# Down projection as 26 block products of a 2x4x4 scheme, with hand-placed SBUF slots and a term preset in PSUM by ScalarE

## The chip, the cores and the metric

The kernel runs on one core of a Trainium2 chip. The metric is the device time of one execution in microseconds. Before: 1897.8 us, the median of three runs (1897.66 to 1897.85).

## The reference

```python
x: (8, 3008, 256)                       # fp32
X = fft(fft(x, axis=1), axis=2).real     # sequence, then features
h = X.reshape(24064, 256) @ w_in         # (256, 2048)
g = maximum(0.01 * h, h)                 # leaky relu
out = g @ w_out                          # (2048, 256)
```

All arithmetic is fp32. The feature transform is linear and is folded into the input weights, so that the kernel computes a cosine and a sine transform along the sequence, and then two projections.

## The kernel before, in words

**Units and chunks.** A unit is one batch entry and one parity of the output frequency (16 units of 752 or 753 frequencies). Each frequency k gives two output rows, k and its mirror, which are the sum and the difference of a cosine half and a sine half. A unit is cut into chunks of 251 or 250 frequencies, 48 in all. The features d and 256 - d are folded, so the cosine and the sine half have 128 features each, and the feature d = 128 is a term of its own: the row `nb` (spread over all partitions) times a weight column `wn`.

**Up.** A step (chunk j, index f of 8) makes two hidden blocks of 128 features. `raised` (L820) issues four matmuls into two PSUM banks, `cos_ps` and `sin_ps`. `activate` then adds the d = 128 term on VectorE (L829, nb times wn plus cos_ps, to SBUF), makes the sum and the difference with sin_ps (L833, L834: the two mirrored rows of `g`), and applies Lrelu on ScalarE (L835). GpSimd makes four sums of column blocks (L842 to L845, tile `s`).

**Down.** `down` (L893) multiplies by a 2x2x2 scheme with seven products for each f, accumulated over all eight f in four PSUM banks. The weights of the products are blocks of w_out (`wo`) and four differences of them (`wt`, made on GpSimd in L601). When the last f is done, seven additions on VectorE (L917) and a copy on ScalarE (L902) make the output tile `o`, and two transfers store it. The first two chunks are "plain" (`down_plain`, L873: eight products for each f), since w_out is still arriving then.

**Sequence transform.** For the next unit, VectorE folds x (L327 to L343) and its rows (L363 to L410) and TensorE makes two groups of eight small matmuls of 94 to 96 columns (L635, `even_rows`, `odd_rows`); `butterfly` puts the parts together on VectorE into the tiles `mix0` and `mix1`, of which there are two each. `dft_direct` does the same for the second unit from the layout of the first load.

**Order.** TensorE and SyncE (SP) follow the order of the program text everywhere, VectorE too but for steps 16 to 22. `step(at)` issues up of step `at` and down of step `at - 3`; folds and transforms are tied to steps by the tables `folds`, `row_folds` and `transforms`. PSUM is two rings of four banks: `up` (also for transforms) and `sum`. SBUF tiles come out of pools with a number of buffers for each tag: five of `g`, four of `s`, two of `o`, two of `nb`. Loads of x, tables and output stores are all issued on SP.

Of the kernel before, what the change touches and what calls it, by code (L numbers as in the profile page):

```python
# [45 lines left out]
SLOPE = 0.01  # L96
# [148 lines left out]
def chunks():  # L245


    out, at = [], 0
    for b in range(B):
        for c in PARITIES:  # L250
            for j in range(0, UW[c], CW):
                n = min(CW, UW[c] - j)
                out.append((b, c, j, n, at))
                at += 2 * n
    return out, at


def columns():

    at = np.zeros(B * S, np.int64)  # L260
    for b, c, j, n, first in chunks()[0]:
        col = j + np.arange(n)
        half, k = col >= KW[c], k_order(c)
        k = np.concatenate([k, k[k != Q]])[col]
        plus, minus = np.where(half, H + k, k), np.where(half, H - k, (S - k) % S)
        at[b * S + minus] = first + n + np.arange(n)
        at[b * S + plus] = first + np.arange(n)
    return at
# [3 lines left out]
def tile_fnet_leaky_relu(  # L272
# [16 lines left out]
    PS = bass.MemoryType.PSUM  # L289
    const = ctx.enter_context(tc.tile_pool(name="const", bufs=1))  # L290
    xp = ctx.enter_context(tc.tile_pool(name="xp", bufs=1))
    work = ctx.enter_context(tc.tile_pool(name="work", bufs=1))
    dram = ctx.enter_context(tc.tile_pool(name="dram", bufs=1, space=bass.MemoryType.DRAM))
    ps = ctx.enter_context(tc.tile_pool(name="ps", bufs=1, space=PS))

    def up_ps(name="up_ps"):
        return ps.tile([P, 512], F32, tag="up", bufs=4, name=name)

    def dft_ps():
        return up_ps("dft_ps")  # L300

    def x_tile():
        return xp.tile([LOADED, 2, 2, NT, D], F32, tag="x", bufs=1, name="xt")

    def sum_ps():
        return ps.tile([P, 512], F32, tag="sum", bufs=4, name="sum_ps")

    def load_x(b):
        t = x_tile()
        for h in range(2):  # L310
            for odd in range(2):
                load_rows(t, b, h, odd)
        return t

    def load_rows(t, b, h, odd):
        nc.sync.dma_start(t[:, h, :, odd * NI[0] : NI[0] + odd * NI[1]], x[b, h, odd])
# [4 lines left out]

    zs = {}
# [22 lines left out]
    def fold_x(b, at):  # L345

        t, rows = xs[b], slice(0, NT)
        h, i = divmod(at, 2)
        if h < 2 and i == 0:
            add_mirrors(t, h, rows)  # L350
        elif h < 2:
            for part in range(2):
                fold_columns(t, h, part, rows)
        else:
            fold_halves(t, i, 3 - h, rows)
        if at == 7:
            zs[b] = xs.pop(b)

    def turn(x, y, a, part, tmp, to, v):
# [3 lines left out]
        nc.scalar.activation(tmp[0], y, ACT.Copy, scale=sin)  # L363
        nc.scalar.activation(tmp[1], y, ACT.Copy, scale=cos)
        if v is nc.vector:
            v.scalar_tensor_tensor(to[0], in0=x, scalar=cos, in1=tmp[0], op0=ALU.mult, op1=op[part])
            v.scalar_tensor_tensor(to[1], in0=x, scalar=sin, in1=tmp[1], op0=ALU.mult, op1=op[1 - part])
            return
        nc.scalar.activation(to[0], x, ACT.Copy, scale=cos)
        nc.scalar.activation(to[1], x, ACT.Copy, scale=sin)  # L370
# [3 lines left out]
    class Rows:  # L374
# [12 lines left out]
        def fold_even(self, v=nc.vector):  # L387
            x, y, z = self.src[:, 2], self.src[:, 3], self.z
            if self.c == 1:
                turn(x, y, 0, self.part, (z(0), z(1)), (z(6), z(7)), v)  # L390
# [6 lines left out]
        def fold_odd(self, v=nc.vector):  # L397
            x, y, z = self.src[:, 4:6], self.src[:, 6:8], self.z
            if self.c == 1:
                for i in range(2):  # L400
                    turn(x[:, i], y[:, i], 1 + i, self.part, (z(2 + 2 * i), z(3 + 2 * i)), (z(8 + 2 * i), z(9 + 2 * i)), v)
# [3 lines left out]
            else:  # L405
# [5 lines left out]
                turn(z(b), z(b + 1), 0, self.part, (z(8), z(9)), (z(10), z(11)), v)  # L411
                self.odd = z(7 - self.part), z(6 + self.part), z(10), z(11)

    def rows_of_x(b, part, c):

        t = zs[b]
        src = t[:, (c + part) % 2, 0, :, part * P : (part + 1) * P]
        return Rows(src, [t[:, part, 1].rearrange("p c (i d) -> p (c i) d", i=2)], part, c)

    class Direct:  # L420
# [14 lines left out]
        def odd_rows(self, m, lo=0, hi=KW[1]):  # L435

            po, n = dft_ps() if m == P else sum_ps(), KW[1]
# [26 lines left out]
    rows_of = {}  # L464

    def fold_rows(u, part, odd):
        if not odd:
            rows_of[u, part] = rows_of_x(u[0], part, u[1])
            rows_of[u, part].fold_even()
        else:  # L470
            rows_of[u, part].fold_odd()


    feat_sb = const.tile([P, 2, 2 * P], F32, name="feat_sb")
    wf = const.tile([P, 2, F], F32, name="wf")
    wn = const.tile([P, NF], F32, name="wn")
    wo = const.tile([P, 2, NH, D], F32, name="wo")
    wt = const.tile([P, 4, NH, P], F32, name="wt")
    nyx = const.tile([LOADED, 2, 2, NT, B], F32, name="nyx")
    nyz = const.tile([LOADED, 16, B], F32, name="nyz")  # L480
    nyf = const.tile([LOADED, 2, 2, 2 * FI, B], F32, name="nyf")
# [6 lines left out]
    def load_tab(n, c):  # L488
        t = const.tile([LOADED, TW[c][n % 2]], F32, name=f"tab_{n}_{c}")
        nc.sync.dma_start(t, seq_tab[n, c, :, 0 : TW[c][n % 2]])  # L490
        tabs[n, c] = t
# [4 lines left out]
    class Weights:  # L496
# [7 lines left out]
        def __init__(self, src, dst):  # L504
            tag = RAW[len(parts)]
            bufs = 1 if tag == "raw" else 2
            words = src.shape[1] * src.shape[2]
            self.raw = work.tile([P, 2 * WN], F32, tag=tag, bufs=bufs, name="raw")[:, 0:words]
            self.dst, self.n = dst, dst.shape[1]
            self.f64 = src.dtype != F32  # L510
            raw = self.raw if not self.f64 else self.raw.bitcast(src.dtype)
            nc.sync.dma_start(raw.rearrange("p (c n) -> p c n", c=src.shape[1]), src)
            parts.append(self)
# [4 lines left out]
        def begin(self):  # L518
# [3 lines left out]
            self.power = work.tile([P, WN], F32, tag="power", bufs=2, name="power")[:, 0 : self.n]  # L522
# [40 lines left out]
    def load_w_in(f0, n, blocks=(0, 1)):  # L563
        words, made = w_in.shape[1] // F, []
        for a in blocks:
            w = work.tile([P, WN], F32, tag="win", bufs=4, name="win")[:, 0:n]
# [4 lines left out]
    def fold_w_in(f0, n, made, tag="up", pieces=1, queue=nc.sync):  # L571


        for w in (1, 0):
            m = n // (1 if w else pieces)
            for at in range(0, n, m):
                pt = ps.tile([P, 512], F32, tag=tag, bufs=4, name="wf_ps")[:, 0:m]
# [12 lines left out]
    def load_w_out(q):  # L590

        src = w_out[q * WB * P : (q + 1) * WB * P, :].rearrange("(c p) d -> p c d", p=P)
        h, f = divmod(q * WB, NH)
        return Weights(src, wo[:, h, f : f + WB, :].rearrange("p c d -> p (c d)"))

    def combine_w_out(f):

        b = [[wo[:, h, f : f + WB, i * P : (i + 1) * P] for i in range(2)] for h in range(2)]
        t = [wt[:, i, f : f + WB, :] for i in range(4)]
        for to, x, y in ((t[0], b[0][1], b[0][0]), (t[1], b[1][1], t[0]), (t[2], b[1][1], b[0][1]), (t[3], b[1][0], t[1])):  # L600
            nc.gpsimd.tensor_tensor(to, x, y, op=ALU.subtract)  # L601
# [37 lines left out]
    def butterfly(to, m, part, c, v=nc.vector, direct=False):  # L639
# [4 lines left out]
        def tile_of(tag, w, bufs=1):  # L644
            return work.tile([P, w], F32, tag=tag, bufs=bufs, name=tag)

        if not direct or v is not nc.vector:
            od = tile_of("od", 568)
        if v is nc.vector:
            ab, ev = tile_of("ab", KC), tile_of("ev", KC, 2)  # L650
# [14 lines left out]
        def copied(bank, at, w):  # L665

            a = work.tile([P, 384], F32, tag="e0", bufs=2, name="e0")
            if v is nc.vector:
# [28 lines left out]
        def added(po, lo=0, hi=kw):  # L697
            if c == 0:
                for lo, hi in ((0, 189), (189, kw)):
                    at = lo + (lo > 0)  # L700
                    nc.vector.tensor_tensor(to[0:m, lo:hi], ev[0:m, lo:hi], po[0:m, at : at + hi - lo], op=ALU.add)
                return
            nc.vector.tensor_tensor(to[0:m, lo:hi], ev[0:m, lo:hi], po[0:m, 0 : hi - lo], op=ALU.add)

        def subtracted(po, lo=0, hi=kw):
            if c == 0:

                last = 283
                for lo, hi in ((0, 189), (189, last), (last + 1, kw)):
                    at, first = lo + (lo > 0), kw + lo - (lo > last)  # L710
                    nc.vector.tensor_tensor(to[0:m, first : first + hi - lo], ev[0:m, lo:hi], po[0:m, at : at + hi - lo], op=ALU.subtract)
                return
            nc.vector.tensor_tensor(to[0:m, kw + lo : kw + hi], ev[0:m, lo:hi], po[0:m, 0 : hi - lo], op=ALU.subtract)

        def odd(po):
            if c == 1:
# [4 lines left out]
                v.tensor_tensor(to[0:m, 0:kw], ev[0:m, 0:kw], od[0:m, 0:kw], op=ALU.add)  # L721
                v.tensor_tensor(to[0:m, kw : UW[c]], ev[0:m, 0:kw], od[0:m, 0:kw], op=ALU.subtract)
# [8 lines left out]
            v.tensor_tensor(to[0:m, 0:kw], ev[0:m, 0:kw], od[0:m, 0:kw], op=ALU.add)  # L731

            last = 283
            v.tensor_tensor(to[0:m, kw : kw + last], ev[0:m, 0:last], od[0:m, 0:last], op=ALU.subtract)
            v.tensor_tensor(to[0:m, kw + last : UW[c]], ev[0:m, last + 1 : kw], od[0:m, last + 1 : kw], op=ALU.subtract)
# [3 lines left out]
    def mix(u, blk, direct=False):  # L739

        t = work.tile([P, UW[0]], F32, tag=f"mix{blk}", bufs=2, name=f"mix{blk}")
        mixed.setdefault(u, {})[blk] = t
        return butterfly(t, P, blk, u[1], direct=direct)

    def dft(u, blk):
        rows = rows_of.pop((u, blk))
# [420 lines left out]
```

## Time and profile before

| | |
|---|---|
| median of the runs | 1897.8 us |
| span of the profiled execution | 1895.3 us |
| TensorE busy, instructions | 1889.2 us, 9088 |
| plain chunks' up steps end | about 109 us |
| first and last down matmul of the 2x2x2 scheme | 129.7 and 1890.5 us |
| 131 to 1890 us: TensorE, VectorE, ScalarE, GpSimd busy | 1759.0, 1161.4, 446.7, 1032.3 us |

The profiled execution's span lies 2.5 us under the median of the runs. The window from 131 to 1890 us is the steady part; before it, weights are loaded and converted, and the first unit is transformed. A matmul in fp32 appears as two instructions of TensorE. In a group's row the number after the bar is the busy time, then the mean of one instruction in ns, then the idle time of that engine just before these instructions and who ended it. Rows of TensorE have durations with the pipeline's depth in them; a rate is read from the starts.

### The profile page before, as it was taken

How to read it: one execution, taken by the hardware profiler on the slowest of the kernel's cores; microseconds unless marked ns; L12 is line 12 of the kernel's file. 1: busy time of each engine (PE TensorE's matmuls, PEld its weight loads, DVE VectorE, ACT ScalarE, POOL GpSimd, SP SyncE). 2: the span in 40 equal slices, each digit the busy share in tenths (PEclk: the TensorE clock that was granted, in tenths of full speed). 3: DMA queues.
4: the chain of work that ended last, by engine and by line, in shares of the span. 5: the costliest groups of instructions: out<-in, count | busy, mean ns of one | idle time of the engine just before them, and what ended most of it. 6: DMA issues, size and time to landing. Idle time of an engine off the chain costs nothing.

```text
span 1895.3 us, 25288 instructions
## 1 busy us (share of the span) xinstructions
PE 1889.2 (100%) x9088; PEld 1682.3 (89%) x9088; DVE 1266.8 (67%) x2543; ACT 501.0 (26%) x674; POOL 1055.5 (56%) x1510
## 2 busy tenths in 40 slices
PE   9999999999999999999999999999999999999999
PEld 7888888988889888898888988889888898888987
DVE  8857765776656776568756687567865677656554
ACT  3522322223222222222222232222322223222222
POOL 0236555565555655556555565555655556555554
PEclk9999999999999999999999999999999999999999
DMA  7312000110002000020000200003000020000000
GB/s 252 114 58 82 12 20 22 51 69 12 31 11 104 16 22 20 12 108 18 16 20 12 108 23 11 20 12 119 12 12 19 17 114 12 20 11 23 12 12 23
DMA packets 34349, 78.74 MB, mean 42 GB/s; under 512 B 5536, under 2 KB 20000, under 8 KB 34224
## 3 DMA queue, kind: packets, MB, share of 16 engines
q1 hardware_dynamic: 33792, 76.86, 10.9%
q8 instruction: 73, 1.20, 0.3%
q14 instruction: 52, 0.43, 0.1%
q10 hardware_dynamic: 432, 0.26, 0.0%
HBM read 52.40 MB, written 24.71 MB: 41 GB/s over the span
## 4 chain that ended last, share of the span: by engine, by line
PE 99%; DVE 0%; issue 0%; ACT 0%; DVEq 0%; POOL 0%; POOLq 0%
PE sum_ps L893 58%; PE sin_ps L820 17%; PE cos_ps L820 17%; PE sum_ps L873 3%; PE dft_ps L635 3%; PE wf_ps L579 1%; PE sum_ps L956 1%; PE dft_ps L431 0%; PE dft_ps L440 0%; PE sum_ps L440 0%; PE dft_ps L458 0%; PE dft_ps L453 0%; DVE cos L829 0%; PE sum_ps L788 0%; DVE wo L545 0%
## 5 line engine op out<-in xcount | busy, mean ns | idle before, releaser
L835 ACT ACTIVATE g<-g 128x1004 f32<-128x1004 f32 (+1 forms) x384 | 399.3, 1040 | 1134.6 <-DVE g L834 1114.4
L829 DVE SCALAR_TENSOR_TENSOR cos<-nb,wn,cos_ps 128x251 f32<-128x251 f32 (+1 forms) x768 | 330.5, 472 | 534.1 <-PE cos_ps L820 531.1
L842 POOL TENSOR_TENSOR s<-g 128x251 f32<-128x251 f32 (+1 forms) x368 | 280.5, 762 | 711.4 <-ACT g L835 705.5
L893 PE MATMUL sum_ps<-s,wt 128*128 128x251 f32 (+1 forms) x2208 | 527.6, 374 | 0.0
L893 PEld LDWEIGHTS sum_ps<-s,wt 128*128 128x128 f32 x2208 | 415.9, 188 | 52.3
L820 PE MATMUL cos_ps<-mix,wf 128*128 128x251 f32 (+1 forms) x1536 | 387.8, 374 | 0.0
L820 PE MATMUL sin_ps<-mix,wf 128*128 128x251 f32 (+1 forms) x1536 | 387.8, 374 | 0.0
L893 PE MATMUL sum_ps<-g,wo 128*128 128x251 f32 (+1 forms) x1472 | 372.8, 375 | 0.0
L820 PEld LDWEIGHTS cos_ps<-mix,wf 128*128 128x128 f32 x1536 | 291.2, 190 | 34.2 <-issue 0.5
L820 PEld LDWEIGHTS sin_ps<-mix,wf 128*128 128x128 f32 x1536 | 290.4, 189 | 34.7
L893 PEld LDWEIGHTS sum_ps<-g,wo 128*128 128x128 f32 x1472 | 277.4, 190 | 31.6
L833 DVE TENSOR_TENSOR g<-cos,sin_ps 128x502 f32<-128x502 f32 (+1 forms) x384 | 260.4, 678 | 52.0 <-DVE cos L829 6.5
L845 POOL TENSOR_TENSOR s<-g,s 128x251 f32<-128x251 f32 (+1 forms) x368 | 259.3, 705 | 28.8
L843 POOL TENSOR_TENSOR s<-s,g 128x251 f32<-128x251 f32 (+1 forms) x368 | 271.9, 739 | 0.0
L834 DVE TENSOR_TENSOR g<-cos,sin_ps 128x502 f32<-128x502 f32 (+1 forms) x384 | 257.5, 671 | 0.0
L844 POOL TENSOR_TENSOR s<-g 128x251 f32<-128x251 f32 (+1 forms) x368 | 256.2, 696 | 0.0
L893 PE MATMUL sum_ps<-s,wo 128*128 128x251 f32 (+1 forms) x736 | 215.8, 375 | 0.0
L893 PE MATMUL sum_ps<-g,wt 128*128 128x251 f32 (+1 forms) x736 | 215.7, 375 | 0.0
L893 PEld LDWEIGHTS sum_ps<-s,wo 128*128 128x128 f32 x736 | 139.5, 190 | 16.3
L893 PEld LDWEIGHTS sum_ps<-g,wt 128*128 128x128 f32 x736 | 139.8, 190 | 15.8
L917 DVE TENSOR_TENSOR o<-e,sum_ps 128x251 f32<-128x251 f32 (+1 forms) x180 | 66.0, 408 | 0.0
L873 PE MATMUL sum_ps<-g,wo 128*128 128x251 f32 x256 | 57.1, 374 | 0.5 <-DVE wo L545 0.5
(130 smaller groups left out, 802.8 us busy)
## 6 DMA issues: line engine op xcount, KB each, us to landing
xt<-in_x_dram SPq DMA_DIRECT2D x28, 1024.0 KB, 7.6
out_dram<-o SPq DMA_DIRECT2D x78, 251.0 KB, 2.3
raw<-in_w_in_dram SPq DMA_DIRECT2D x8, 512.0 KB, 5.8
raw<-in_w_out_dram SPq DMA_DIRECT2D x8, 512.0 KB, 4.5
out_dram<-o SPq DMA_DIRECT2D x16, 250.0 KB, 2.1
xt<-in_first_x_dram SPq DMA_DIRECT2D x4, 768.0 KB, 8.4
nb<-nyq_dram SPq DMA_DIRECT2D x8, 376.5 KB, 3.4
nb<-nyq_dram SPq DMA_DIRECT2D x7, 376.0 KB, 4.5
```

The source lines that it names most:

```text
L820: nc.tensor.matmul(pt[blk][:, h * n : (h + 1) * n], lhsT=wf[:, blk, fs[h] * P : (fs[h] + 1) * P], rhs=mixed[b, c][blk][:, at : at + n], st ...
L829: nc.vector.scalar_tensor_tensor(cos[:, hs], in0=spreads[b, c][:, at : at + n], scalar=wn[:, fs[h] : fs[h] + 1], in1=pt[0][:, hs], op0=ALU ...
L833: nc.vector.tensor_tensor(g[:, 0], cos[:, 0 : 2 * n], pt[1][:, 0 : 2 * n], op=ALU.add)
L834: nc.vector.tensor_tensor(g[:, 1], cos[:, 0 : 2 * n], pt[1][:, 0 : 2 * n], op=ALU.subtract)
L835: nc.scalar.activation(g, g, ACT.Lrelu)
L842: nc.gpsimd.tensor_tensor(s1, a[1][0], a[1][1], op=ALU.add)
L843: nc.gpsimd.tensor_tensor(s2, s1, a[0][0], op=ALU.subtract)
L844: nc.gpsimd.tensor_tensor(s3, a[0][0], a[1][0], op=ALU.subtract)
L845: nc.gpsimd.tensor_tensor(s4, a[0][1], s2, op=ALU.subtract)
L873: nc.tensor.matmul(sums[j][d][:, r * n : (r + 1) * n], lhsT=wo[:, fs[h] // NH, fs[h] % NH, d * P : (d + 1) * P], rhs=a[r][h], start=(f == ...
L893: nc.tensor.matmul(sums[j][p], lhsT=still[p], rhs=moving[p], start=(f == 0 and i % 2 == 0), stop=(f == NH - 1), skip_group_check=True)
L917: nc.vector.tensor_tensor(to, x, y, op=ALU.add)
```

## The change

- **Down.** A chunk and the next one of equal width are taken together, as a "four": 31 in all, 22 of width 188, eight of 189, one of 125. Their four column blocks (two chunks, two mirrored rows) by four row blocks of the hidden layer by two halves of the output are multiplied with 26 products in place of 32. Each product is four matmuls (g = 0 to 3), and all four stand next to each other in the list. 28 sums of hidden blocks (table `SUMS`) are made on GpSimd, each over all four g at once; 18 sums of weights (`W_SUMS`) once, on GpSimd. Two results of products share a PSUM bank; there are three banks for them. As soon as a bank is complete, `combine` copies some of it on ScalarE and adds the rest on VectorE (34 additions a four), and the eight outputs are stored one by one.
- **Up.** One stage of `Four.up` is one block of 128 hidden features over both chunks of the four (376 or 378 columns): two matmuls. `seed` has ScalarE write nb times wn into the cos bank ahead of the matmul, two stages early; the matmul then adds to it. ScalarE copies the cos bank to SBUF; VectorE makes the sum and the difference with the sin bank (`hidden`), each straight into two slots; ScalarE applies Lrelu, in place.
- **Memory.** `block_sb` has 23 slots of 4 x 189 columns for hidden values and their sums, handed out by a free list in the order of the program; `part_sb` has 22 for outputs. The same memory holds the buffers of the start. x takes three parts of eight rows in place of four, and the tables of the transform are loaded anew for each unit. `mix` and `nb` become rings of three halves.
- **Order.** All five engines follow the order of the program text, from the start to the end. `rest` makes one list of events with due times in "steps" (16 to a four): up at 1.6 + 0.9 f, sums at the times of `SUMS`, products at 17 + m/6.5. VectorE's combinations (`soon`) and folds (`later`) are queued and given out by `spare` in front of and after each up stage, some 0.8 us at a time.
- **Last four.** Every third sum is on VectorE.

```diff
+    def seed(self, f):
+        n = 2 * self.n
+        nc.scalar.activation(cos_ps[f % 2][:, 0:n], columns_of(nb_sb, ...), ACT.Copy, scale=wn[:, f : f + 1])
+    def up(self, f):
+        for i, bank in enumerate((cos, sin)):
+            nc.tensor.matmul(bank[:, 0:n], lhsT=wf[:, i, f * P : (f + 1) * P], rhs=columns_of(mix_sb[i], ...),
+                             start=(i == 1), stop=True, skip_group_check=True)
...
+        nc.scalar.copy(copy, cos[:, 0:n])
+    def hidden(self, k, g, copy, sin):
+        cols = slice(g * n, (g + 1) * n)
+        for r in range(2):
+            a, b = self.at[4 * k + r], self.at[4 * k + 2 + r]
+            step = b - a
+            end = b + (1 if step > 0 else -1)
+            tos.append(block_rows[:, a : (None if end < 0 else end) : step, cols])
...
+        for to, op in zip(tos, (ALU.add, ALU.subtract)):
+            nc.vector.tensor_tensor(to, x, y, op=op)
+    def sum(self, i, engine=None):
+        x, y, sign, _ = SUMS[i]
+        free = [s for s in (self.used(x), self.used(y)) if s is not None]
+        self.at[16 + i] = free.pop(0) if free else block.take()
+        (engine or nc.gpsimd).tensor_tensor(self.value(16 + i), xa, ya, op=ALU.add if sign > 0 else ALU.subtract)
+        for s in free:
+            block.drop(s)
...
+    def product(self, q, g):
+        nc.tensor.matmul(to, lhsT=weight(w)[:, g], rhs=self.value(v)[:, g * n : (g + 1) * n],
+                         start=(first and at == 0), stop=(last and g == 3), skip_group_check=True)
...
+            else:
+                made = four.up(i)
+                seed(16 * t + i + 2)
+                spare(0.8)
+                for to in four.hidden(*made):
+                    nc.scalar.activation(to, to, ACT.Lrelu)
+                spare(0.9)
-        nc.vector.scalar_tensor_tensor(cos[:, hs], in0=spreads[b, c][:, at : at + n], scalar=wn[...], in1=pt[0][:, hs], ...)
-        nc.vector.tensor_tensor(g[:, 0], cos[:, 0 : 2 * n], pt[1][:, 0 : 2 * n], op=ALU.add)
-        nc.vector.tensor_tensor(g[:, 1], cos[:, 0 : 2 * n], pt[1][:, 0 : 2 * n], op=ALU.subtract)
-        nc.gpsimd.tensor_tensor(s1, a[1][0], a[1][1], op=ALU.add)
-        nc.gpsimd.tensor_tensor(s2, s1, a[0][0], op=ALU.subtract)
-        nc.gpsimd.tensor_tensor(s3, a[0][0], a[1][0], op=ALU.subtract)
-        nc.gpsimd.tensor_tensor(s4, a[0][1], s2, op=ALU.subtract)
```

## Prediction

> **What bounds the kernel now.** I read the page's busy times and slices first, then the groups, then the waits, then two stretches of the timeline.
>
> ```profile
> PE 1889.2 (100%) x9088; PEld 1682.3 (89%) x9088; DVE 1266.8 (67%) x2543; ACT 501.0 (26%) x674; POOL 1055.5 (56%) x1510
> ...
> PEclk9999999999999999999999999999999999999999
> ```
>
> TensorE never rests and has its full clock. A matmul in fp32 stands as two instructions ("passes"); the end of the chain, 54 passes of 251 columns in 11.47 us, gives 0.212 us a pass. The prices of other widths come from three rows of the TensorE timeline, by their starts:
>
> ```profile
> 114.83 0.80 PE L453 MATMUL dft_ps<-direct,xt 128*128 128x380 f32 x2
> 115.47 0.81 PE L458 MATMUL dft_ps<-direct,xt 126*128 126x188 f32 x4
> 116.12 1.01 PE L820 MATMUL cos_ps<-mix,wf 128*128 128x250 f32 x4
> ```
>
> Two passes of 380 take 0.64, so 0.32 each; four of 188 to 192 take 0.65, so 0.16 each. Narrow passes aren't held up by their weight loads.
>
> ```profile
> L835 ACT ACTIVATE g<-g 128x1004 f32<-128x1004 f32 (+1 forms) x384 | 399.3, 1040 | 1134.6 <-DVE g L834 1114.4
> L829 DVE SCALAR_TENSOR_TENSOR cos<-nb,wn,cos_ps 128x251 f32<-128x251 f32 (+1 forms) x768 | 330.5, 472 | 534.1 <-PE cos_ps L820 531.1
> L842 POOL TENSOR_TENSOR s<-g 128x251 f32<-128x251 f32 (+1 forms) x368 | 280.5, 762 | 711.4 <-ACT g L835 705.5
> ...
> L834 DVE TENSOR_TENSOR g<-cos,sin_ps 128x502 f32<-128x502 f32 (+1 forms) x384 | 257.5, 671 | 0.0
> ```
>
> The other engines wait for each other in a ring, and it costs nothing: GpSimd waits 706 us for Lrelu, ScalarE 1114 us for VectorE, VectorE 531 us for TensorE. One turn of it:
>
> ```profile
> 608.92 0.67 DVE L834 TENSOR_TENSOR g<-cos,sin_ps 128x500 f32<-128x500 f32 x1
> 609.70 1.04 ACT L835 ACTIVATE g<-g 128x1000 f32<-128x1000 f32 x1 [4.88 <-DVE g L834]
> ...
> 610.82 0.63 POOL L842 TENSOR_TENSOR s<-g 128x250 f32<-128x250 f32 x1 [2.79 <-ACT g L835]
> ```
>
> A hand-over costs about 0.1 us (609.59 to 609.70, 610.74 to 610.82). The changed kernel depends on how dear GpSimd is:
>
> ```profile
> L842 POOL TENSOR_TENSOR s<-g 128x251 f32<-128x251 f32 x304 | 240.3, 791 | 560.5 <-ACT g L835 560.5
> ...
> L601 POOL TENSOR_TENSOR wt<-wo 128x256 f32<-128x256 f32 x8 | 5.8, 728 | 34.9 <-DVE wo L545 34.9
> ...
> L406 POOL TENSOR_TENSOR nyz<-nyx 95x16 f32<-95x16 f32 x1 | 0.2, 217 | 0.0
> ```
>
> From 16 to 256 elements it rises by 511 ns: 2.13 ns an element over 0.18 us.
>
> [...] of one L842 shape the median is 711 ns and the mean 791; over all 1472 sums the excess is 53 us for 143 us of overlap with such instructions, 0.37 us for each. [...]
>
> **The change on TensorE.** After the two plain chunks, before has 46 chunks of 88 matmuls: 1716 us (8096 passes by 0.212). After has 31 "fours". Down: 2288 matmuls of 188 columns, 832 of 189, 104 of 125; two passes each, at 0.160 (0.112 for 125): 1021 us. Up: 704 of 376, 256 of 378, 32 of 250: 621 us with 0.317 and 0.212. Sum 1642, so TensorE loses 74 us. The sequence transform is unchanged. A four of 188 costs 208 x 0.160 + 64 x 0.317 = 53.5, with its share of the transform (16 passes at 0.111) 55.3 us.
>
> **VectorE and ScalarE.** VectorE loses the wn products (L829) and gets per four 32 TENSOR_TENSOR of 376 from PSUM at 0.54 (between 0.409 for 251 in L917 and 0.675 for 502), 34 combinations at 0.345, and its old folds: about 37 of 55 us. ScalarE gets 16 seeds (about 0.6), 16 copies (0.47, as L789), 32 Lrelus at 0.52 (L835's 1.04 less 628 x 0.82 ns, the slope of its copies), 8 copies: about 39 of 55. Both lie beside TensorE if each is in time. Output goes out as 8 transfers a four in place of 4 in two chunks, on SP, behind table loads; SP is nearly idle and I cost that at nothing (up to 20 us if loads of x land late).
>
> **GpSimd.** It makes 28 sums per four: 607 of 752 elements at 1.785 us, 224 of 756 at 1.79, 28 of 500 at 1.25; together 1520 us. That is 50 of the 55.3 us of a four, so any wait beyond 5 us a four sets the end.
>
> **The waits that the change adds.** I read them from the changed kernel's instruction order. `hidden` writes two slots of one large block with one strided access. Only 80 of the 992 such writes have neighbouring slots; in the others up to 20 slots lie between. The order shows that such a write waits for sums that wrote a slot in between, and such a sum for the Lrelu of slots around it: the stretch counts, not the two slots. So the ring of before comes back between fours that share no data. At 202 of the 859 sums GpSimd's next sum waits for a Lrelu whose TENSOR_TENSOR pair waited for the sum just before; nothing else stands between the two in GpSimd's order. The price of one: 0.54 + 0.54 + 0.52 and four hand-overs (0.35) = 1.95 us where it waits for the first Lrelu (71 places), 2.5 for the second (131). In 10 of them a whole further up stage lies between (copy 0.47, two TENSOR_TENSOR, two Lrelu, hand-overs: 2.95). Sum 138 + 328 + 30 = 496 us. At 60 more places one sum can run meanwhile: about 35 us. Behind GpSimd wait the products, then the PSUM banks; behind VectorE's waiting write stand combinations and folds (1.2 us an up stage), which fit beside the sums that run then.
>
> **Start, contention, end.** The plain steps end at 109 us (L820). Their two last downs take 7; then 15 ups of the first four, with nothing to overlap, go at 0.37 + 2 x 0.41 + 2 x 0.42 + 0.35 = 2.4 us each, and dft_direct and the Nyquist rows stand between: first sum at about 155. VectorE's two-SBUF work is about 300 us; with 80% of it over sums, at 0.37: 85-90. Fours in which TensorE is the longer: 20. Last products, combinations, store: 6.
>
> Sum: 155 + 1520 + 496 + 35 + 87 + 20 + 6 = 2319 us of span. The profiled execution before has a span of 1895.3 against a median of 1897.8; with that 2.5, 2320.
>
> **Bounds.** Sums: among the 251s some operand offsets give 630 ns, others 718. At the fast rate a 752 costs 1.52, in all 230 us less. I take the slow one[...]. Contention: 40 to 170. Start: 145 to 170. A hand-over of 0.05 or 0.15: 40 us either way. Side work on VectorE that isn't covered: 0 to 240.
>
> **Rivals.**
> - *TensorE still sets the end* (faster). One mechanism: the waits are in time, because GpSimd runs ahead. It decides if they cost under 5.3 us a four. For it: a product stands about 1.5 ups after its sum. Against it: 496 us over 30 fours is 16.5. It gives 1897.8 - 74, plus 12 for the start that overlaps nothing and 5 at the end (sums are late when no ups are left): 1841.
> - *Fast sums*: 2320 - 230 = 2090. For it: 432 of the 1472 present sums run at that rate (L844 of the 251s, two lines of the 250s). Against it: L601's 728.
> - *The ring catches side work too*: VectorE's 1.2 us per up stage comes in the way at each of the 202 places: 2320 + 242 = 2560. Against it: only some 80 of 480 stages hold more than the sums beside them cover.
> - *The change doesn't do what it says*: the order shows 26 x 4 products a four, so no.
>
> **Numbers.** Forecast 0.69; fast sums 0.10; more of the ring 0.13; TensorE-bound 0.06; something near the old time 0.02. The range, 2080 to 2500, takes in the fast sums and leaves out the TensorE-bound case and half of the worst one. Slower by over 0.2% (what a measurement can tell from none) 0.93, faster 0.05, same 0.02.
>
> **What would show it.** TensorE busy at about 75%, its idle time ended by GpSimd's sums; GpSimd as the longest engine at 1.6 ms or more, waiting some 500 us for Lrelu; Lrelu waiting for the TENSOR_TENSOR pair and this for sums; a sum of 752 at 1.8 us; passes of 188 at 0.16. The forecast is wrong if TensorE is again at 99%, or if GpSimd's idle time is under 150 us.

## The result and the profile after

| | |
|---|---|
| median of the runs, before and after | 1897.8 and 2449.0 us |
| ratio after/before, 95% interval | 1.290 [1.288, 1.292] |
| span of the profiled execution after (its own time 2446.3) | 2444.6 us |
| forecast, range | 2320, 2080 to 2500 us |

The change makes the kernel 29% slower. The page of the changed kernel first; its rows answer to the busy times and slices shown of before.

```profile
PE 2025.6 (83%) x9424; PEld 1659.9 (68%) x9424; DVE 1573.0 (64%) x2820; ACT 1130.4 (46%) x2490; POOL 1606.7 (66%) x900
...
PEclk9998999989999898988998989999998988899999
```

TensorE is no longer full (83% against 100%), and its clock, at nine tenths or more in every slice before, now falls in many slices (mean 0.925). No engine is full: something makes them take turns. The groups of the changed kernel say who waits (busy time and mean ns of one, then the idle time ahead and who ended it):

```profile
L1038 POOL TENSOR_TENSOR block<-block 128x752 f32<-128x752 f32 (+2 forms) x859 | 1576.0, 1853 | 741.7 <-ACT block L1208 535.1 <-PE sum_psc L1053 76.6 <-PE cos_psb L999 42.2
L1208 ACT ACTIVATE block<-block 128x376 f32<-128x376 f32 (+2 forms) x992 | 495.9, 514 | 837.4 <-DVE block L1021 824.5 <-ACT block L1208 0.4
L921 DVE TENSOR_TENSOR part<-part 128x188 f32<-128x188 f32 (+2 forms) x403 | 381.2, 970 | 4.3
...
L1021 DVE TENSOR_TENSOR block<-cos,sin_psb 128x376 f32<-128x376 f32 (+2 forms) x496 | 258.2, 539 | 313.2 <-POOL block L1038 230.2 <-PE sin_psb L999 39.8 <-ACT cos L1006 38.2
```

GpSimd's sums wait 535 us for Lrelu, Lrelu 825 us for VectorE's pair of writes, the pair for sums: the ring that was harmless before is closed, and this time with TensorE outside it. From the waits of the changed kernel (us in total, times, longest):

```profile
ACT block L1208 <- DVE block L1021: 824.5, 466, 7.9
POOL block L1038 <- ACT block L1208: 535.1, 224, 8.3
DVE block L1021 <- POOL block L1038: 377.0, 186, 4.9
...
PE sum_psc L1053 <- POOL block L1038: 200.3, 76, 7.5
```

TensorE's products wait at the end of it. One turn of the ring in the timeline of the changed kernel, GpSimd, then VectorE, then ScalarE (start, duration):

```profile
1284.90 3.50 POOL L1038 TENSOR_TENSOR block<-block 128x752 f32<-128x752 f32 x2 [2.40 <-ACT block L1208]
1290.86 10.69 POOL L1038 TENSOR_TENSOR block<-block 128x752 f32<-128x752 f32 x6 [2.46 <-ACT block L1208]
```

```profile
1288.44 1.12 DVE L1021 TENSOR_TENSOR block<-cos,sin_psb 128x376 f32<-128x376 f32 x2 [3.98 <-POOL block L1038]
```

```profile
1289.66 1.06 ACT L1208 ACTIVATE block<-block 128x376 f32<-128x376 f32 x2 [3.86 <-DVE block L1021]
```

The sums end at 1288.40; the pair of additions takes 1288.44 to 1289.56, the pair of Lrelus 1289.66 to 1290.72, and the next sum starts at 1290.86, after 2.46 us in which GpSimd does nothing. The forecast had 2.5 for this place. Where a sum waits for the first Lrelu alone, the gap is 1.85 us (at 1325.93 and 1338.70 in the same stretch); the forecast had 1.95.

The sums' records add up to the span: the first starts at 150.0 us, all 859 on GpSimd take 1592 us, the gaps between them, less 16 us of overlap, 697 us, and 6.5 us follow the last one: 2445.

### The profile page after: what moved, and what is told of

It reads as the page before. It is cut to its first block, busy times and chain, and to the rows that moved or that the text cites. A ratio compares the mean times of both kernels' runs of the same rounds, so it can differ in the third digit from the quotient of the medians.

```text
span 2444.6 us, 27317 instructions
## 1 busy us (share of the span) xinstructions
PE 2025.6 (83%) x9424; PEld 1659.9 (68%) x9424; DVE 1573.0 (64%) x2820; ACT 1130.4 (46%) x2490; POOL 1606.7 (66%) x900
## 5 line engine op out<-in xcount | busy, mean ns | idle before, releaser
L1038 POOL TENSOR_TENSOR block<-block 128x752 f32<-128x752 f32 (+2 forms) x859 | 1576.0, 1853 | 741.7 <-ACT block L1208 535.1
L1208 ACT ACTIVATE block<-block 128x376 f32<-128x376 f32 (+2 forms) x992 | 495.9, 514 | 837.4 <-DVE block L1021 824.5
L1021 DVE TENSOR_TENSOR block<-cos,sin_psb 128x376 f32<-128x376 f32 (+2 forms) x496 | 258.2, 539 | 313.2 <-POOL block L1038 230.2
L1021 DVE TENSOR_TENSOR block<-cos,sin_psa 128x376 f32<-128x376 f32 (+2 forms) x496 | 257.4, 537 | 260.9 <-POOL block L1038 146.8
L1053 PE MATMUL sum_psa<-block,wt 128*128 128x188 f32 (+2 forms) x1736 | 342.0, 334 | 54.3 <-POOL block L1038 53.9
L921 DVE TENSOR_TENSOR part<-part 128x188 f32<-128x188 f32 (+2 forms) x403 | 381.2, 970 | 4.3
L1053 PEld LDWEIGHTS sum_psa<-block,wt 128*128 128x128 f32 x1736 | 296.8, 196 | 117.1 <-POOL block L1038 71.5
L1053 PE MATMUL sum_psc<-block,wt 128*128 128x188 f32 (+2 forms) x1736 | 324.1, 329 | 48.7 <-POOL block L1038 48.5
L1053 PEld LDWEIGHTS sum_psc<-block,wt 128*128 128x128 f32 x1736 | 290.2, 195 | 82.6 <-POOL block L1038 57.7
L999 PE MATMUL cos_psa<-mixc,wf 128*128 128x376 f32 (+2 forms) x496 | 209.1, 505 | 2.1 <-ACT cos_psa L993 2.1
```

Source lines behind the costliest of these rows:

```text
L921: self.push(n / 960 + 0.15, lambda: nc.vector.tensor_tensor(to, x, y, op=op), tag)
L999: nc.tensor.matmul(bank[:, 0:n], lhsT=wf[:, i, f * P : (f + 1) * P], rhs=columns_of(mix_sb[i], self.u, self.j, n), start=(i == 1), stop=Tr ...
L1021: nc.vector.tensor_tensor(to, x, y, op=op)
L1038: (engine or nc.gpsimd).tensor_tensor(self.value(16 + i), xa, ya, op=ALU.add if sign > 0 else ALU.subtract)
L1053: nc.tensor.matmul(to, lhsT=weight(w)[:, g], rhs=self.value(v)[:, g * n : (g + 1) * n], start=(first and at == 0), stop=(last and g == 3), ...
L1208: nc.scalar.activation(to, to, ACT.Lrelu)
```

## The experiments

**Theory.** The ring through falsely shared stretches of the block memory sets the time: a strided access over two slots is ordered against everything between the slots, so sums, pair writes and Lrelus of unrelated data wait in turn. **Rivals**: the waits are those of real data (a sum needs its Lrelu) and stay when the stretches are gone; or the sums themselves, with what they do to VectorE, set the time.

The first four kernels change the stretches; the two cuts also make more and shorter instructions of the same work. The cut of the Lrelu (A) and the cut of the pair write (B):

```diff
 A           for to in four.hidden(*made):
-                nc.scalar.activation(to, to, ACT.Lrelu)
+                for i in range(2):
+                    nc.scalar.activation(to[:, i], to[:, i], ACT.Lrelu)
 B           for to, op in zip(tos, (ALU.add, ALU.subtract)):
-                nc.vector.tensor_tensor(to, x, y, op=op)
+                for i in range(2):
+                    nc.vector.tensor_tensor(to[:, i], x[:, i], y[:, i], op=op)
```

**Cut A alone: Lrelu slot by slot.**

> The Lrelu over a pair of slots is cut into two, one slot each (1984 in place of 992; the same work otherwise). In the instruction order 92 in place of 320 sums then wait for a Lrelu, and none of the 202 places is left where a sum waits for a Lrelu whose TENSOR_TENSOR pair waited for the sum just before. My theory (the ring of waits over stretches between slots): GpSimd's 535 us of waiting for Lrelu go, its waits for TensorE stay at most as they are (139 us), TensorE's clock returns: 1850 to 1930 us, although ScalarE has some 190 us more to do. Rival, GpSimd's 28 sums a four are too many in themselves: its 1592 us stay and other waits take the place, 2300 us or more. Rival, ScalarE's queue (seed, copy, Lrelu) is what is late: slower than 2449 us, since it gets more instructions.

Measured: 2289.1 us, ratio 1.206 [1.204, 1.208]. The theory's number was missed by over 350 us. The waits of this kernel say why:

```profile
ACT block L1209 <- DVE block L1021: 653.3, 451, 8.9
POOL block L1038 <- DVE block L1021: 400.4, 238, 6.0
```

Sums no longer wait for Lrelu, but they wait for VectorE's pair of additions, whose output has the very same stretch. One cut shortens each turn by the Lrelu (400.4 / 238 = 1.68 us in place of 535.1 / 224 = 2.39), and the ring stays closed.

**Cut B alone: pair write slot by slot.**

> Only VectorE's sum and difference are cut into one slot each; the Lrelu keeps the pair. The order still has 195 of the 202 places, since the Lrelu of the pair waits for the sum. My theory: the ring stands, no gain, 2430 to 2520 us (VectorE has 0.15 us more at 32 places a four, in the ring). Rival, it is VectorE's wait for GpSimd (377 us) that costs: 2100 us or less.

Measured: 2282.6 us, 1.204 [1.201, 1.206]; faster than the theory's range by some 150 us, and far from the rival's. Now the Lrelu pair alone keeps the ring, also with shorter turns (1.74 us on the mean, without the 30.1 us ahead of the very first sum):

```profile
POOL block L1039 <- ACT block L1209: 418.7, 224, 30.1
...
ACT block L1209 <- POOL block L1039: 168.7, 137, 3.7
```

**Both cuts.**

> Both cut. None of the 202 places is left; VectorE and ScalarE both have more instructions. My theory: as with the Lrelu alone within 2%, 1850 to 1940 us. Rival, VectorE's own waits for stretches matter beside the ring: clearly faster than with the Lrelu alone.

Measured: 2105.7 us, 1.110 [1.108, 1.111]. Of all that the change loses (551 us), 343 go with the two cuts; either alone takes some 160. The instruction order of this kernel has none of the 202 places left, and the trace agrees; its waits:

```profile
ACT block L1210 <- DVE block L1022: 528.6, 224, 14.0
POOL block L1039 <- PE sum_psc L1054: 300.9, 68, 8.6
PEld sin_psa L999 <- DVE block L1022: 147.3, 48, 4.7
...
POOL block L1039 <- ACT block L1210: 34.6, 2, 29.5
```

GpSimd waits for Lrelu twice, one of them the first sum of all. So the ring of false waits is real, and cutting it gains 343 us. But the theory's time for this kernel (up to 1940) was missed, and it is clearly faster than with the Lrelu cut alone, as the rival had it: 535 us of waits gone should have given more. Another wait has come in: sums wait for TensorE, whose products have yet to read the slot that the sum goes into; TensorE waits for VectorE's additions to empty its banks. VectorE is 84% busy here, and one group of it has become dear:

```profile
PE 1902.2 (90%) x9424; PEld 1583.7 (75%) x9424; DVE 1774.8 (84%) x3812; ACT 1194.9 (57%) x3482; POOL 1639.9 (78%) x900
```

```profile
L921 DVE TENSOR_TENSOR part<-part 128x188 f32<-128x188 f32 (+2 forms) x403 | 486.2, 1231 | 4.3
```

1231 ns for an addition of 188 columns, where the same with one operand in PSUM takes about 345. That is the second theory: **VectorE's instructions with two SBUF operands are held while GpSimd works**, called the lock theory below (the lock is a name for this holding, no more).

**Near slots: the two slots of a pair taken as close as the free list allows** (82 of the 202 places left).

```diff
-                for j in range(4):
-                    self.at[4 * k + j] = block.take()
+                for r in range(2):
+                    x, y = min(((x, y) for x in block.free for y in block.free if x < y), key=lambda p: p[1] - p[0])
+                    ...
+                    self.at[4 * k + r], self.at[4 * k + 2 + r] = x, y
```

> The four slots of a group are picked from the free ones as two pairs with the fewest slots between; instructions as in the changed kernel. The order has 82 of the 202 places left. My theory: the waits for Lrelu shrink in proportion, by 535 x 120/202 = 318 us, so 2130 us, 2050 to 2200. Rival (the number of instructions on VectorE and ScalarE, or GpSimd's rate, sets the time): 2400 us or more, since neither changes.

Measured: 2259.9 us, 1.191 [1.189, 1.193]; missed by 60 us over the range.

```profile
POOL block L1041 <- ACT block L1211: 367.5, 121, 13.1
```

The waits fall from 224 to 121, but each is longer (3.04 us in place of 2.39). A count of places by one price is not enough once the stages between them shift.

**Near slots, and only the pairs that are not neighbours cut** (508 of 992), to see if the additional instructions of the two cuts cost anything.

> Slots picked as near pairs, and only those pairs cut that aren't neighbours (508 of 992): no false wait is left, with 484 fewer instructions on VectorE and on ScalarE than with all cut. Theory (VectorE sets the end now): its 0.15 us for each of 484 are saved nearly in full, 2020 to 2090 us. Rival, GpSimd or ScalarE sets it: within 1% of 2106.

Measured: 2123.3 us, 1.119 [1.117, 1.121]: within 1% of both cuts, as the rival said. So 484 fewer instructions each on VectorE and ScalarE gain nothing here; the slots differ too, so what the number alone is worth was not measured.

**Both cuts, and sums of 64 columns.** The sum's line becomes `m = 4 * self.n if self.u < 2 else 64` and `tensor_tensor(to[:, 0:m], xa[:, 0:m], ya[:, 0:m])`, so that most columns of the sums are left out.

> Both pairs cut, as in the third experiment, and from the third unit on (28 of 31 fours) GpSimd's sums cover 64 of 752 columns: most of the block sums are left out. Theory now: with the ring gone (2106 us), VectorE is held up, since an instruction of VectorE with two SBUF inputs waits while a sum of GpSimd runs; a part<-part addition of 188 columns took 1572 ns over a sum and 348 ns beside none. Then these fall under 500 ns in the mean, TensorE sets the pace at 55 to 57 us a four, and the time is 1890 to 1960 us. Rival, VectorE's work as such (84% busy, many instructions) holds TensorE up: 2050 us or more.

Measured: 1862.6 us, 0.982 [0.980, 0.983]. The short additions and the full TensorE are as the theory has it; the time lies 28 us under its range. Page and VectorE group of this kernel:

```profile
PE 1826.0 (98%) x9424; PEld 1545.9 (83%) x9424; DVE 1253.6 (67%) x3812; ACT 1226.1 (66%) x3482; POOL 434.7 (23%) x900
```

```profile
L921 DVE TENSOR_TENSOR part<-part 128x188 f32<-128x188 f32 x286 | 97.1, 365 | 3.0
```

With the same order and the same instructions TensorE is full again, and the part additions are back from 1218 ns (188 columns, both cuts) to 365. The waits are not quite the same: a sum of 64 columns touches only the front of its slots, so that in the instruction order 306 of the 859 sums wait for an earlier product or Lrelu than with both cuts. With that reservation, what is left after the two cuts, 243 us, hangs on the sums' length. It doesn't say whether through GpSimd's own time or through what it does to VectorE.

**Both cuts, and each sum in two halves** (`for cols in (slice(0, 2 * self.n), slice(2 * self.n, 4 * self.n))`): the same work on GpSimd, with twice the chances for VectorE to come in between.

> Both pairs cut, and each sum of GpSimd made in two instructions of half the columns (0.18 us more each, 5 us a four on GpSimd). If VectorE waits for the end of the GpSimd instruction that runs, the wait halves with it: a part<-part addition of 188 over a sum falls from 1572 ns to 800 to 1000, and the time to 1930 to 2060 us. Rival, the two engines share the bandwidth and the length of an instruction doesn't matter: 1572 ns stays, and the time is 2106 us or more, up to 2250.

Measured: 2147.3 us, 1.133 [1.130, 1.135]; worse than with whole sums, and in the rival's range. But the rival's 1572 ns did not stay: the usual held addition of 188 columns got shorter (those over 0.4 us have a median of 1.65 us with whole sums and 1.04 here), and 15 of the 403 wait far longer, 205 us of the 502 that all of them take. VectorE and then GpSimd in the timeline of this kernel:

```profile
1081.16 13.69 DVE L921 TENSOR_TENSOR part<-part 128x188 f32<-128x188 f32 x1
1094.77 1.12 DVE L1022 TENSOR_TENSOR block<-cos,sin_psb 128x188 f32<-128x188 f32 x4
```

```profile
1075.79 18.84 POOL L1041 TENSOR_TENSOR block<-block 128x376 f32<-128x376 f32 x20
```

One addition of 188 columns takes 13.69 us: it stands through a run of twenty half sums that follow each other without a gap, and ends with the run (1094.6 and 1094.8). This is not the rule: 284 other part additions that met a half sum ended some 0.21 us after it, with the next half sum following just as closely. What tells the 15 from the 284 stays open. All two-SBUF work of VectorE together takes as long as with whole sums (1017 and 1005 us).

**The changed kernel, ring and all, with VectorE's two-SBUF instructions cut to 8 columns** from the ninth four on (`to, x, y = (a[..., 0:8] for a in (to, x, y))` for parts and x); the other columns of these combinations and folds are left out.

> The changed kernel with its ring (all 202 places), but from the ninth four on VectorE's additions with two SBUF inputs on the output parts and on x cover 8 columns of each row: most of the combination and folding is left out, the number of instructions stays. If VectorE waits for the end of a running sum whatever its own length, these still take over 1 us in the mean over a sum, and the time falls little: 2380 to 2450 us. Rival, the excess over my forecast is the columns that VectorE moves at a shared rate: 2300 to 2350 us, near the sum of the ring.

Measured: 2344.1 us, 1.235 [1.233, 1.237]; the time is the rival's. But the instructions behave as the lock theory has it:

```profile
L925 DVE TENSOR_TENSOR part<-part 128x8 f32<-128x8 f32 x316 | 184.0, 607 | 3.4
```

In their records an 8-column addition takes about 1.0 us on the mean where it lies wholly over sums, and 160 ns beside none, so that 8 columns in place of 188 shorten it by a third only (from 1.45 us). The order of waits on the four computing engines is that of the changed kernel. Against it the sums are 50 us shorter and the gaps 58 us: the columns of VectorE's side work are worth about 105 us in the changed kernel, half of it as longer sums, half as longer waits. The short instructions still wait, and the first eight fours have the whole work, so this is not all that the side work costs.

**Can the load be placed better?** Four kernels with both cuts move it. If the lock were all, taking the held work off VectorE should help, and so should taking sums off GpSimd.

All 403 part additions on GpSimd (`nc.gpsimd.tensor_tensor(to, xa, ya, op=op)` in their place in the order):

> Both pair writes are cut per slot as before, and all 403 combinations with two SBUF operands (part<-part) are moved from VectorE to GpSimd, where they stand in program order among the sums. Theory (VectorE instructions with two SBUF operands are held while GpSimd works, and that sets the end of the kernel with both cuts, 2106 us): VectorE loses about 570 us of held work; GpSimd then has 28 x 1.785 + 13 x 0.58 = 57.5 us a four, so the time is 155 + 30 x 57.5 + 6 and some waits: 1900 to 1990 us, GpSimd busy near 1.8 ms, idle time of GpSimd that TensorE's products end falls from 301 us to under 120. Rival (it is not the lock but the order of sums, products and combinations as such that makes GpSimd wait for TensorE): GpSimd now waits for products at the combinations too, the sums queue behind, and the time is 2080 us or more.

Measured: 2187.7 us, 1.151 [1.149, 1.154]; the rival was right. GpSimd's waits in this kernel:

```profile
POOL part L1094 <- DVE part L921: 171.1, 86, 10.4
...
POOL block L1039 <- PE sum_psc L1054: 23.0, 18, 5.8
```

The sums' wait for TensorE fell from 301 to 23 us as the theory had it, and VectorE from 84% to 63% busy; but GpSimd works in order, and a part addition waits there for VectorE's additions and they for the products, with the next sums queued behind.

155 of them, where the expectation says 150:

> As the run with all 403 combinations on GpSimd, but only 150 of them moved. Theory (the held VectorE work sets the end): VectorE loses 37% of the held work, GpSimd has about 53 us a four: 1990 to 2060 us, between the kernel with both cuts (2106) and the one with all of them moved. Rival (waits of GpSimd for products): no gain over 2106, or a loss that grows with the number moved.

Measured: 2110.1 us, 1.111 [1.109, 1.113]: no gain over both cuts, again as the rival said.

Every second sum on VectorE (`four.sum(i, nc.vector if i % 2 else None)`), and every third (`i % 3 == 2`):

> Both pair writes are cut per slot, and every second sum (14 of 28 of a four) is made on VectorE in place of GpSimd, at the same place in the program's order. A VectorE sum of 752 that is not held should take about 0.93 us (0.347 for 188, rising by the 1.04 ns an element between 188 and 251 to 502 columns from PSUM). Theory (VectorE's work with two SBUF operands and GpSimd's sums exclude each other, and this set the end of the kernel with both cuts): the two together then need 14 x 1.78 + 14 x 0.93 + 8 = 46 us of a four in place of 58, below TensorE's 55: GpSimd is busy for about 0.85 ms, additions of part by part of 188 columns average under 800 ns, and the time is 1850 to 1960 us, possibly below the kernel before. Rival (the order of sums and products makes the engines wait for each other whatever GpSimd's share): VectorE, in order, now waits for the Lrelu of each sum's operands, pair writes queue behind it, and the time stays at 2050 us or more.

> As the run with every second sum on VectorE, but every third (9 of 28). Theory (exclusion): 19 x 1.78 + 9 x 0.93 + 8 = 50 us of a four: 1900 to 2010 us, between the run with every second one and 2106. Rival (waits of order): within 1% of 2106 or above.

Measured: 2083.7 us, 1.098 [1.096, 1.099], and 2114.4 us, 1.113 [1.112, 1.115]. The theory's times were missed and the rival's met. With every second sum moved, the theory's two signs came all the same: GpSimd is busy for 858 us, and part additions of 188 columns take 742 ns on the mean. The page of that kernel, and its longest wait:

```profile
PE 1894.6 (91%) x9424; PEld 1568.5 (75%) x9424; DVE 1896.4 (91%) x4237; ACT 1191.7 (57%) x3482; POOL 858.1 (41%) x475
```

```profile
POOL block L1039 <- DVE block L1039: 775.8, 149, 11.7
```

GpSimd idles and VectorE is full. My sum for these runs (46 us a four) counted what the two engines exclude each other from, and forgot VectorE's own PSUM work: the pair additions alone are 64 by 0.34 = 22 us a four. A sum of 752 columns on VectorE also takes 1211 ns on the mean here and not 930 (936 at the median of the nine in the changed kernel), as is to be expected where GpSimd's sums still hold it. So neither account fits whole: the time is the rival's, but VectorE is late through its own work. With all of the computation in it, no version came below the kernel before.

## Why the forecast held, and where it was short

The sign was right, and so was the main mechanism, the ring of false waits with GpSimd in order. A second one, VectorE held up by the sums, was put at nothing. Step by step:

- **False waits (202 places, 496 us, and 35 us for 60 more).** Right: 224 waits for Lrelu, 535 us, against 531. The prices of one turn were 2.5 and 1.95 us and are 2.46 and 1.85 in the turns shown. That the sums agree to 4 us is luck in part: the forecast has 262 places at 2.03 us on the mean, the trace 224 waits at 2.39, and with the side work cut to 8 columns these 224 take 504 us. Both cuts remove the waits, so that their cause is shown, not only argued. What the forecast did not say is that either pair, the additions' or the Lrelus', closes the ring alone.
- **Sums (1520 us) with contention (87 us).** 1592 against 1607. A sum of 752 columns beside no such VectorE instruction takes 1778 ns, as forecast (1.785).
- **First sum (155), tail (6).** 150.0 and 6.5.
- **"Fours where TensorE is longer" (20 us).** This is the mis-sized term of the sum. What is in the gaps beside the waits for Lrelu is 697 - 535 = 162 us: 111 us in which TensorE ended the wait (77 from the products' third bank, 34 from the up stages' banks, without the first sum's wait), 35 of issue, 15 others.
- **VectorE's side work "fits beside the sums" (0, bound 0 to 240), contention on GpSimd alone.** This is the assumption behind it, and it was wrong. I took the 0.37 us for each us in which a sum of the kernel before overlaps VectorE's two-SBUF instructions (53 us for 143), and did not look at the other side. It stood in that trace:

```profile
L722 DVE TENSOR_TENSOR mix<-ev,od 128x376 f32<-128x376 f32 x14 | 13.7, 978 | 0.0
...
L735 DVE TENSOR_TENSOR mix<-ev,od 128x93 f32<-128x93 f32 x14 | 10.7, 765 | 0.0
...
L731 DVE TENSOR_TENSOR mix<-ev,od 128x377 f32<-128x377 f32 x14 | 8.0, 573 | 0.5
```

In the kernel before, 93 columns took 765 ns on the mean, 376 took 978 and 377, at another place, 573: a price that hardly goes with the width hints at waiting. The runs show the waiting for VectorE. An addition of 188 columns with two SBUF operands takes 348 ns beside no sum and about 1.45 us wholly over sums in the changed kernel; additions with an operand in PSUM stay at about 345. In all, such work of VectorE takes 833 us in the changed kernel and 462 with short sums, so the forecast's 300 us for it was far too small.

How much of the 142 us that are missing in the gaps (162 against 20) this makes is shown in small part: with the side work cut to 8 columns the gaps fall by 58 us, 31 of them in the waits for Lrelu and 27 in the others. No run takes the other 115 us apart; the 8-column instructions still wait, and TensorE's clock, below, is another candidate. The sum of the differences is -5 for the start, -15 for the sums, +4 for the waits for Lrelu and +142 for the others: 126. With 2 us more between span and median, and the forecast rounded to 2320, that is the 129 us to 2449.

- **Rivals.** TensorE setting the end was given 1841 us: with both cuts and sums of 64 columns the kernel does just that, at 1862.6, with passes of 188 columns 0.159 us and of 376 columns 0.316 us apart. So the loss isn't in the products; 26 products for 32 would have paid about 2% without the ring and with sums that cost next to nothing. Fast sums (630 ns for 251): no, 1778 ns for 752. In the kernel before the rate goes by line and width (medians: L842 711 ns at 251 columns and 627 at 250, L844 632 and 714); whether the operands' offsets decide it, as the forecast assumed, was not tested. The ring catching side work (2560) was the direction in which the forecast erred, at about half of its size.
- **What was to show it.** GpSimd waiting for Lrelu, Lrelu for the pair, the pair for sums: seen. GpSimd as the longest engine at 1.6 ms: its busy time is 1607 us, but TensorE's records add up to 2026 us (83%, not 75%), some of it at a lower clock.

**What stays open.** With both cuts the kernel stands at 2106 us, 243 over that with short sums. GpSimd (78% busy), VectorE (84%) and TensorE (90%) then hold each other up in turn, as their waits suggest: a held part addition delays the pair additions behind it, these TensorE's next up stage, that the products queued behind it, and these the sums that write into their slots. Moving work from VectorE to GpSimd or back only made another of the three late. No run tells which part of the 243 is this holding and which is GpSimd's plain time. Pairs of slots reserved as neighbours, which would need no cuts, were not tried.

An estimate, not a measurement, points to the holding. It steps through each kernel's instruction order, with durations that these traces show for instructions that nothing holds (348 ns for 188 columns with two SBUF operands, some 1775 for a sum of 752, 159 for a pass of 188) and a hand-over set at 0.06 us. With the rule that a sum and a two-SBUF instruction of VectorE shut each other out, it gives 2453 us for the changed kernel, 2114 for both cuts and 1849 for short sums, where the spans are 2445, 2106 and 1860. It misses the half sums by 108 us, since it has no long holds, and the four kernels that move load by up to 4%. Without the rule it gives 2248, 1843 and 1824. By this estimate GpSimd's plain time adds next to nothing to the kernel with both cuts, the other waits of the kernel with short sums are worth 5 us, and in the changed kernel the holding costs about 200 us, where the forecast had 87.

## What to carry to other kernels

A strided access over two tiles is ordered here against everything between them (224 waits of sums for Lrelu, 535 us; with both cuts two), so before packing values into one large buffer, count in the instruction order which waits run through addresses that share no data; and remember that each access with such a stretch closes the ring alone. Price the sharing of GpSimd and VectorE on both engines: look up VectorE's rows with two SBUF operands at several widths, and where the mean hardly depends on the width (here 765 ns for 93 columns, 978 for 376), add the rest of the other engine's running instruction to its price. A saving on the busiest engine (a forecast 74 of 1890 us on TensorE) is only had if the second engine's new load (here 50 of each 55 us, in order) leaves room for its waits.

## What the runs showed of the hardware that was not expected

- **VectorE can be shut out for many instructions.** With half sums, 15 part additions were held until fourteen more half sums had followed, 13.7 us each, while 284 came in at the first end. With whole sums the part additions of the changed kernel took at most 1.97 us; with all part additions on GpSimd, three other two-SBUF instructions of VectorE were held for 6.6 to 7.3 us, one of them in an unbroken run of seven sums.
- **GpSimd loses less.** A sum of 752 columns takes 1778 ns beside no two-SBUF instruction of VectorE and 1933 on the mean where one overlaps it; all sums together lose about 78 of 1592 us. The longest, 2781 ns, runs beside a fold of 1024 columns, and the 49 that overlap folds of 1024 or 1016 columns take 2405 on the mean: a long instruction of VectorE holds GpSimd up in its turn.
- **TensorE's clock halves after gaps.** In the changed kernel's record the granted clock is either full or half, and half for 368 us in 78 stretches, 73 of them of 3.4 or 6.8 us. There, 338 of some 4200 intervals between neighbouring passes of 188 columns lie, most at 0.31 us in place of 0.159: about 52 us of TensorE's time. With both cuts there are 102 such, with short sums none. The idle time ahead need not be unbroken. With the stretches' own 3.4 us as the window, 74 of the 78 follow one in which TensorE was busy for 46% or less by its records, 11 of them for 0%, while of 529 such windows inside full clock three lie under 45%. How much of it reached the end was not measured; the estimate above puts it at about 6 us.
